# Adaptive layernorm, dilated local attention and SwiGLU on one core: a new instruction order from a search that uses delays read from the trace

## The chip, the cores and the metric

The kernel runs on one core of a Trainium2 chip. The core has a matrix engine (PE; its weight loads are shown apart as PEld), a vector engine (DVE), a scalar engine (ACT), a general one (POOL) and a queue engine (SP) that issues nearly all transfers of this kernel. Each runs its own instructions in the order in which they were written and waits for the others through semaphores. The metric is the time of one execution on the device in microseconds (us); lower is better.

## The reference

One layer over 2048 positions of 512 values: a conditioning vector gives six modulation vectors; then layernorm, attention, residual, layernorm, gated feed-forward (FFN), residual.

```python
x = A_x
mod = (_silu(c) @ w_mod).reshape(c.shape[0], 6, 1, -1)
sa, ca, ga, sb, cb, gb = ...
h = _layernorm(x, axis=-1) * (1 + ca) + sa
x = x + ga * _A_ref(h, A_wqkv, A_wo)      # 32 heads of 16; each position sees itself and
                                          # the positions 2, 4, ... 14 before it (W=8, dil=2)
h = _layernorm(x, axis=-1) * (1 + cb) + sb
x = x + gb * _B_ref(h, B_w1, B_w3, B_w2)  # (silu(h @ w1) * (h @ w3)) @ w2, F = 1792
```

## The kernel before

The positions are cut into 16 tiles of 128 (T = 0 to 15). `_build` records 1118 operations, each with an engine, what it reads and writes, and pools of buffers. `Program.place` then puts them in the order that the list ORDER gives (numbers of operations, over all engines) and gives each pooled value the buffer that SLOTS names; `synchronize` works out the waits from that, also the one for the last user of a buffer that is taken again; `emit` writes each engine's operations in that order. So ORDER and SLOTS decide everything about the schedule: nothing is reordered at run time. GATES adds three waits to late weight loads.

Names used below, with the lines where the work is issued:

- Opening: 24 warm-up matmuls (L518), the modulation columns (L504, L487), two blocks of gate columns (L531, weights `wm_g`) and their spreading over partitions (L541), whose results scale `wo` (L946, DVE) and `w2` (L952).
- First layernorm, QKV groups of tiles [0,1], [2,3], [4-7], [8-11], [12-15]: statistics on DVE (L555, L556), the power on POOL (L565), the normalised tile on DVE (L571, L576, called nm), then a transpose: on PE with an eviction by ACT (L636, L644) for the first three groups, by a transfer (L124) with a modulation by ACT in place (L621) for the last two. The result is `h`.
- Projections (PE): q and k (L691) in pieces q0 to q19 and k0 to k19, v (L711) by tile; ACT evicts them (L700, L701, L721). v goes through one of three buffers to DRAM (`v_scratch`), from where it is read back shifted (eight rows per position) into `vsh`, four transfers per tile (vl).
- Attention by pairs of tiles: products of q and shifted k on DVE (L742, pq), their sums over each head by PE (L752, lg, in a quarter of the columns per matmul), maximum, subtraction (L764, L769), exponential on ACT (L782), sum, reciprocal, product on DVE (L794, L796, L797), a transpose on PE (L807, at) that ACT evicts (L811), products with v on DVE (L827, av), their sum on PE (L855, ac, a quarter of the columns again), eviction by ACT (L861), a transposing transfer (ot), `wo` on PE (L867) and the residual on DVE (L871, rs), which also gives the sum for the second layernorm.
- Second layernorm, FFN groups 0 to 5 of tiles [0,1], [2,3], [4-7], [8-11], [12,13], [14,15]: mean on POOL (L586), squares on ACT (L590), the rest on POOL (L596, L597, L599), normalisation on ACT (L601), transposes on PE for groups 0 and 1, by transfers (tr14 to tr20) and L621 for the others.
- FFN: 14 blocks per group, numbered f0 to f83; each has four matmuls for the gate and four for the up part (L883; 256 or 512 positions wide), a silu on ACT (L889) and a product on DVE (L892). Two halves of seven matmuls per tile (L921, z) give the output, four of 10 and 4 for the last two tiles (L909); DVE adds x (L931) and SP stores it (zo).

PSUM has eight banks, one per matmul result in flight, so a late eviction holds up a later matmul that takes its bank.

Of the kernel before, what the change touches and what calls it, by code (L numbers as in the profile page):

```python
# [272 lines left out]
def _build(p, A_x, A_wqkv, A_wo, B_w1, B_w3, B_w2, c, w_mod, out):  # L273
# [752 lines left out]
]  # L1026
SLOTS = [
# [48 lines left out]
```

## Time and profile before

| what | us |
|---|---|
| runs shown: median (lowest to highest) of 3 | 243.57 (243.03 to 244.15) |
| the profiled execution, its time | 242.82 |
| its span, first to last instruction | 241.1 |
| PE busy / idle in the span | 230.4 / 10.7 |
| DVE busy | 179.6 |
| ACT busy | 138.7 |
| mean granted clock of PE | 1.0 |

In the rows, "sb_x<-sb_y" is what is written and read, "x8" how many instructions, and what stands in brackets is the idle time of that engine before the row and what ended it. Rows that merge several instructions of one line give their start and their length. A few matmul records are missing, which shows as a row with one matmul fewer than its block has. "SPq" is SP's queue: its rows show the issue of a transfer, not its landing.

### The profile page before, as it was taken

Reading aid. Unit: us, or ns where it says so; the run is one execution under the profiler, and the core shown is the slowest. Engines: PE = TensorE matmul, PEld = TensorE weight load, DVE = VectorE, ACT = ScalarE, POOL = GpSimd, SP = SyncE. Lnnn points to the kernel's source line nnn. Section 1 sums busy time; section 2 is a strip of 40 time slices with the busy share of each in tenths; the row PEclk is TensorE's granted clock in tenths of the full one; section 3 lists DMA queues with packets and bytes.
Section 4 is the critical chain, followed back from the end, with each engine's and each line's share of the span. In section 5 each row is a group of like instructions: output and inputs, shape, how many; then the busy total and the mean of one; then the engine's idle time right before and its main releaser. Section 6 shows DMA issues by size and latency. Waiting matters only on the chain.

```text
span 241.1 us, 4538 instructions
## 1 busy us (share of the span) xinstructions
PE 230.4 (96%) x1781; PEld 136.8 (57%) x1806; DVE 179.6 (75%) x279; ACT 138.7 (58%) x267; POOL 30.9 (13%) x66
## 2 busy tenths in 40 slices
PE   7988999979999999999799999999999999999995
PEld 4856454544587685564345444444565584485874
DVE  5697999979989999898999999764565044423542
ACT  2296497688999744955964578646537253140300
POOL 4332060004001000250005301001001000000000
PEclk9999999999999999999999999999999999999999
DMA  6999999999979996693893882253220300000103
GB/s 222 370 327 327 163 262 234 287 282 343 331 134 253 283 270 115 160 272 99 213 256 119 195 197 46 66 141 98 76 79 0 46 0 0 3 22 0 48 0 109
DMA packets 46317, 38.85 MB, mean 161 GB/s; under 512 B 21704, under 2 KB 37080, under 8 KB 46296
## 3 DMA queue, kind: packets, MB, share of 16 engines
q1 hardware_dynamic: 46288, 38.56, 62.5%
q8 instruction: 14, 0.23, 0.4%
q14 instruction: 7, 0.06, 0.1%
q10 hardware_dynamic: 8, 0.00, 0.0%
HBM read 29.62 MB, written 4.21 MB: 140 GB/s over the span
## 4 chain that ended last, share of the span: by engine, by line
PE 50%; ACT 1%; DMA 1%; issue 1%; DVE 0%; SPq 0%
PE pall L883 30%; PE pall L921 12%; PE pall L867 3%; PE pall L909 3%; DMA sb_h<-sb_xn 1%; ACT sb_h L621 1%; PE pall L855 1%; PE pall L752 1%; PE pall L807 0%; ACT sb_al L811 0%; DVE sb_o L931 0%; SPq L124 0%
## 5 line engine op out<-in xcount | busy, mean ns | idle before, releaser
L883 PE MATMUL pall<-sb_h,sb_w 128*128 128x256 bf16 (+1 forms) x665 | 101.8, 307 | 1.0 <-ACT sb_h L621 0.6
L883 PEld LDWEIGHTS pall<-sb_h,sb_w 128*128 128x128 bf16 x672 | 64.8, 98 | 36.2 <-issue 1.5
L892 DVE TENSOR_TENSOR sb_hh<-sb_sg,pall 128x256 bf16<-128x256 bf16 (+1 forms) x84 | 40.4, 505 | 32.1 <-PE pall L883 32.0
L889 ACT ACTIVATE sb_sg<-pall 128x256 bf16<-128x256 f32 (+1 forms) x84 | 36.2, 455 | 43.4 <-PE pall L883 37.3
L921 PE MATMUL pall<-sb_w,sb_hh 128*128 128x512 bf16 x189 | 43.7, 379 | 0.4
L742 DVE TENSOR_TENSOR sb_pq<-sb_q,sb_kT 128x4096 bf16<-128x4096 bf16 x16 | 36.3, 2282 | 0.0
L921 PEld LDWEIGHTS pall<-sb_w,sb_hh 128*128 128x128 bf16 x196 | 19.1, 98 | 21.0
L691 PE MATMUL pall<-sb_h,sb_wqkv 128*128 128x512 bf16 (+1 forms) x159 | 30.3, 336 | 0.1
L827 DVE TENSOR_TENSOR sb_vsh<-sb_vsh,sb_al 128x4096 bf16<-128x4096 bf16 x12 | 27.3, 2286 | 2.4 <-ACT sb_al L811 2.2
L621 ACT ACTIVATE sb_h<-sb_h,sb_modc 128x512 bf16<-128x512 bf16 (+1 forms) x24 | 16.3, 733 | 13.0 <-DMA sb_h<-sb_xn 13.0
L691 PEld LDWEIGHTS pall<-sb_h,sb_wqkv 128*128 128x128 bf16 x160 | 15.1, 98 | 12.2 <-ACT sb_h L644 0.5
L931 DVE TENSOR_TENSOR sb_o<-pall,sb_x 128x512 bf16<-128x512 f32 (+1 forms) x18 | 10.9, 627 | 11.8 <-PE pall L921 8.7
L586 POOL TENSOR_SCALAR sb_nm<-sb_sx 128x2 f32<-128x2 f32 x8 | 3.7, 465 | 115.9 <-DVE sb_x L871 115.9
L590 ACT ACTIVATE sb_xn<-sb_x,sb_nm 128x512 bf16<-128x512 bf16 x16 | 11.4, 714 | 11.7 <-POOL sb_nm L586 11.7
L867 PE MATMUL pall<-sb_wo,sb_ot 128*128 128x512 bf16 x60 | 15.0, 379 | 1.1 <-DMA sb_ot<-sb_ac 0.5
L711 PE MATMUL pall<-sb_wqkv,sb_h 128*128 128x512 bf16 x58 | 15.0, 379 | 0.3 <-issue 0.2
L644 ACT ACTIVATE sb_h<-pall,sb_modc 128x256 bf16<-128x256 bf16 (+1 forms) x18 | 9.9, 616 | 8.6 <-DVE sb_modc L509 6.7
L601 ACT ACTIVATE sb_xn<-sb_x,sb_nb,sb_rs 128x512 bf16<-128x512 bf16 x16 | 12.6, 806 | 3.7 <-POOL sb_nb L599 3.7
L871 DVE SCALAR_TENSOR_TENSOR sb_x<-pall,sb_x 128x512 bf16<-128x512 f32 x16 | 11.0, 688 | 2.3 <-PE pall L867 2.3
L701 ACT ACTIVATE sb_kT<-pall 128x512 bf16<-128x512 f32 x16 | 9.6, 606 | 4.7 <-PE pall L691 4.7
L555 DVE BATCH_NORM_STATS2 sb_st<-sb_x 128x6 f32<-128x512 bf16 x16 | 10.4, 678 | 1.3 <-DMA sb_x<-in_A_x_dram 1.3
L721 ACT ACTIVATE sb_v<-pall 128x512 bf16<-128x512 f32 x16 | 9.6, 612 | 2.4 <-DMA v_scratch_dram<-sb_v 2.3
(87 smaller groups left out, 208.6 us busy)
## 6 DMA issues: line engine op xcount, KB each, us to landing
sb_vsh<-v_scratch_dram SPq DMA_DIRECT2D x48, 256.0 KB, 4.6
sb_vshx<-v_scratch_dram SPq DMA_DIRECT2D x16, 256.0 KB, 4.3
sb_w<-in_B_w_dram SPq DMA_DIRECT2D x6, 512.0 KB, 5.6
sb_w<-in_B_w_dram SPq DMA_DIRECT2D x6, 384.0 KB, 6.0
v_scratch_dram<-sb_v SPq DMA_DIRECT2D x16, 128.0 KB, 5.9
out_dram<-sb_o SPq DMA_DIRECT2D x14, 128.0 KB, 1.9
sb_wqkv<-in_A_wqkv_dram SPq DMA_DIRECT2D x6, 256.0 KB, 6.0
sb_x<-in_A_x_dram SPq DMA_DIRECT2D x4, 256.0 KB, 6.3
```

The lines of the kernel that those rows point to most:

```text
L590: p.op("act", lambda e, vn=vn, T=T: e.activation(vn.at[:], x_sb[:, T, :], ACT.Square, bias=nm[:, T, :], accum_out=var[:, T, :]), c_act(512 ...
L601: p.op("act", lambda e, vn=vn, T=T: e.activation(vn.at[:], x_sb[:, T, :], ACT.Identity, bias=nb[:, T, :], scale=rs[:, NT + T, :]), c_act(5 ...
L621: return e.activation(vh.at[:, ft, 0:n * P], vh.at[:, ft, 0:n * P], ACT.Identity, bias=modc[:, 8 * which + ft:8 * which + ft + 1], scale=m ...
L691: ins = e.matmul(bank(vp)[:, j * n:(j + 1) * n], wqkv[:, t, col:col + P], vh.at[:, t, 0:n], start=(t == ORDER[0] and j == 0), stop=(t == O ...
L711: ins = e.matmul(bank(vp), vh.at[:, t, tt * P:(tt + 1) * P], wqkv[:, t, 2 * D:3 * D], start=(t == ORDER[0]), stop=(t == ORDER[-1]))
L742: return e.tensor_tensor(vp.at[:], in0, in1, ALU.mult)
L827: return e.tensor_tensor(v_w, v_w, a_w, ALU.mult)
L867: ins = e.matmul(bank(vy), vt.at[:, ft, :], wo[:, ft, :], start=(ft == 0), stop=(ft == KT - 1))
L883: ins = e.matmul(bank(vp)[:, 0:n], wt[:, t, fi * P:(fi + 1) * P], vh.at[:, t, 0:n], start=(t == 0), stop=(t == KT - 1))
L889: p.op("act", lambda e: e.activation(vt.at[:, 0:n], bank(vgp)[:, 0:n], ACT.Silu), c_act(n), k, r=[vgp], w=[vt], table="silu")
L892: p.op("dve", lambda e: e.tensor_tensor(vh_.at[:, 0:n], vt.at[:, 0:n], bank(vup)[:, 0:n], ALU.mult), c_dve(n), k, r=[vt, vup], w=[vh_])
L921: ins = e.matmul(bank(vz), vhh[fi].at[:, tt * P:(tt + 1) * P], w2[:, fi, :], start=(fi == 0), stop=(fi == NF - 1))
```

## The change

ORDER and SLOTS are replaced; all else is the same text, GATES included. Each engine issues the same instructions with the same shapes. The list was found by a search that began at the old one and reckoned with delays and late transfers read from the old order's trace.

```diff
@@ GATES, ORDER and SLOTS @@
 GATES = [-1, -1, -1, -1, -1, -1, -1, -1, -1, 1, -1, -1, -1, -1, -1, 1, -1, -1, 2, -1]
 ORDER = [
     8, 9, 10, 0, 20, 21, 22, 3, 4, 1, 2, 16, 17, 23, 24, 25, 26, 27, 28, 29, 30, 31, 32, 34, 33, 18, 59, 60, 61, 62, 63, 64, 11, 12,
-    13, 65, 55, 19, 56, 5, 6, 7, 57, 58, 66, 67, 68, 69, 70, 71, 72, 73, 74, 75, 76, 77, 78, 79, 80, 81, 82, 91, 38, 92, 93, 94, 96,
-    97, 98, 99, 95, 101, 35, 14, 105, 83, 100, 84, 42, 40, 85, 102, 106, 86, 103, 104, 87, 39, 89, 88, 141, 143, 142, 144, 145, 90,
+    13, 65, 55, 19, 56, 5, 36, 6, 7, 57, 58, 66, 67, 68, 69, 70, 71, 72, 73, 74, 75, 76, 77, 78, 79, 80, 81, 82, 91, 38, 92, 93, 94,
+    96, 97, 98, 99, 95, 101, 35, 14, 105, 83, 100, 84, 42, 40, 85, 102, 106, 86, 103, 104, 87, 39, 89, 88, 15, 141, 124, 119, 120,
...
 ]
 SLOTS = [
-    7, 0, 1, 2, 3, 4, 5, 6, 0, 1, 2, 3, 4, 5, 6, 0, 7, 1, 2, 3, 4, 5, 6, 0, 7, 3, 4, 5, 6, 0, 1, 1, 0, 2, 0, 0, 7, 3, 4, 6, 1, 2, 0,
+    7, 0, 1, 2, 3, 4, 5, 6, 0, 1, 2, 3, 4, 5, 6, 7, 0, 1, 2, 3, 4, 5, 6, 7, 0, 3, 4, 5, 6, 0, 1, 1, 0, 2, 3, 0, 4, 0, 7, 1, 0, 2, 1,
...
```

What this means on the engines, at the places that the prediction speaks of (operations by the names above, in their order on that engine):

```
PE, between the two blocks of gate columns (L531)
  before  transposes of tr4 and tr5, k4, q6, v2, then L531
          (L636 x10, L691 256-wide x16, L711 x4)
  after   q6, v3, spread of gate 1, q4, k10, k9, q8, then L531
          (L691 256-wide x8, L711 x4, L541 x4, L691 256-wide x8, L691 512-wide x12)
SP    before  x12-15, wo, wo, wm_g of block 2, ...
      after   x12-15, wo, wo, wo, wm_g of block 2, ...
SP    before  tr6, v2, tr6, w1, vl0, tr6, tr6, vl0 ... vl1
      after   v2, tr6 x4, then vl1 and vl0 mixed, eight in a row
PE    before  lg5, lg4, wo0, wo1, k17, q17, ...   (QKV group of tiles 12 to 15 begins with k17)
      after   lg4, lg5, q12, wo0, wo1, k16, q16, ...
ACT   before  ac0, ac1, tr9, tr9, tr9, k14, v7, k15, tr9, v9, v8, q14, exp of tiles 2 and 3
      after   ac0, ac1, v10, q14, k14, tr9, v8, k13, tr9, tr9, q12, tr9, exp of tiles 2 and 3
SP    after   tr8, tr8, tr8, v6, w1, ot0, v10, ot1
              (v6 frees the buffer that v8 takes; tr9 is the eviction of tr8)
POOL  before  FFN group 2: var of pair 1, power, product, mean of pair 2, ...
      after   mean of pair 2 stands before the power of pair 1
PE, unbroken stretches of L752 and L855
  before  (lg1 lg0) (lg2 ac0 lg3 ac1) (lg5 lg4) (lg6 ac3 lg7 ac2) (ac5) (ac4 lg8 lg9 ac7 ac6)
          (ac9 lg11 lg10 ac8) (lg12 ac10 lg13 ac11) (lg14 lg15) (ac13 ac12) (ac15 ac14)
  after   (lg0 lg1) (lg2 ac0 lg3 ac1) (lg4 lg5) (lg6 ac3) (lg7 ac2) (lg9 ac5) (lg8 ac4) (ac7) (ac6)
          (ac9 lg11 lg10 ac8) (ac11 lg12 lg13 ac10) (lg14 lg15) (ac13 ac12) (ac15 ac14)
DVE   before  av13, av12, sums, av14, rs13, rs12, f43, zo5, av15
      after   av13, f41, av12, zo2, zo6, rs13, rs12, av15, av14
SP    before  vl14, ot13, ot12, vl15 x4, tr18, tr18, zo6, zo7, ot15, ot14
      after   vl15, vl12, ..., ot13, ot12, vl14 x4, tr18, tr18, ot15, ot14
PE    after   wo13, wo12, f47, f47, f54, f46, f46, z11, ac15, ac14, f51, f54, z15, f43, f44, wo14
```

120 rows, old and new, of tables (ORDER, SLOTS) are left out of this document.

## The prediction

> **What bounds the kernel now.** I read the page's first two parts first, then the engines' busy time by stretch, PE's waits, and PE's timeline around each wait.
>
> ```profile
> PE 230.4 (96%) x1781; PEld 136.8 (57%) x1806; DVE 179.6 (75%) x279; ACT 138.7 (58%) x267; POOL 30.9 (13%) x66
> ```
>
> ```profile
> 8.43:62.20 53.77, 50.40 (x441) 28.21 (x450) 48.99 (x80) 41.20 (x77) 11.57 (x19) 1.00 1.13 284
> 62.20:116.50 54.30, 52.16 (x489) 34.99 (x493) 51.31 (x70) 39.99 (x80) 6.18 (x12) 1.00 0.83 211
> 116.50:178.50 62.00, 61.42 (x395) 30.04 (x402) 49.71 (x62) 38.37 (x69) 7.98 (x12) 1.00 0.55 136
> 178.50:238.49 59.99, 59.69 (x394) 38.76 (x397) 24.05 (x50) 17.58 (x41) 1.30 (x4) 1.00 0.08 22
> ```
>
> (Columns: stretch, length, then busy time of PE, PEld, DVE, ACT, POOL; granted clock; DMA share, GB/s.) PE sets the end at full clock. It is idle 3.37 us before 62.2, 2.14 in the next stretch, 0.58 and 0.30 in the last two. Operations stay the same, so a new order can only win back those 5.5 us in the first two, and can lose anywhere. DVE is idle only 54.30 - 51.31 = 2.99 us in the second stretch: a second bound close behind.
>
> ```profile
> 18.10 0.54 PE L531 MATMUL pall<-sb_csT_bf,sb_wm_g 128*128 128x1 bf16 x16 [0.63 <-DMA sb_wm_g<-in_w_mod_dram]
> 22.71 0.54 PE L531 MATMUL pall<-sb_csT_bf,sb_wm_g 128*128 128x1 bf16 x16 [0.88 <-DMA sb_wm_g<-in_w_mod_dram]
> 49.47 1.06 PE L752 MATMUL pall<-sb_pq,sb_E 128*32 128x256 bf16 x32 [0.85 <-ACT sb_kT L701]
> 50.99 1.67 PE L867 MATMUL pall<-sb_wo,sb_ot 128*128 128x512 bf16 x7 [0.46 <-ACT sb_h L621]
> 65.59 0.40 PE L807 MATMUL pall<-sb_ident,sb_attn 128*128 128x128 bf16 x4 [0.18 <-ACT sb_sg L889]
> 96.84 1.02 PE L867 MATMUL pall<-sb_wo,sb_ot 128*128 128x512 bf16 x4 [0.51 <-DMA sb_ot<-sb_ac]
> 115.33 0.61 PE L855 MATMUL pall<-sb_vsh,sb_ind 128*32 128x512 bf16 x8 [0.67 <-DVE sb_vsh L827]
> 116.50 5.99 PE L883 MATMUL pall<-sb_h,sb_w 128*128 128x512 bf16 x27 [0.55 <-ACT sb_h L621]
> ...
> 149.31 6.04 PE pall L921 x28
> ```
>
> These are PE's real waits (the number in brackets). A 512-wide matmul occupies 6.04 / 28 = 0.216 us. Where a row has one matmul too few (x7 of 8, x27 of 28), the unrecorded first one fills 0.216 of the gap, so 0.46 is 0.24 and 0.55 is 0.33. Together: gates 1.51, the 49-51 us pair 1.09, the four later ones 0.18 + 0.51 + 0.67 + 0.33 = 1.69. After 116.5 PE has nothing to win.
>
> **The change, part by part.** Only ORDER and SLOTS differ: the same instructions in another order on each engine and SP, in other buffers.
>
> **1. Gate columns (L531).** Between the two gate blocks stood ten transposes, sixteen 256-wide and four 512-wide projection matmuls; now sixteen 256-wide (0.108 each), four spreads and sixteen 512-wide: 1.7 + 0.2 + 3.5 = 5.4 us. From about 18.5 the second block is reached near 23.9; its weights landed at 22.71. One more piece of wo is now ahead of them on SP (128 KB at the stretch's 284 GB/s, an estimate of 0.46 us), which still fits: 0.88 is gone. The first block has two more transposes ahead, so 0.5 of its 0.63 may stay. Gain 1.0 (bounds 0.4 to 1.5).
>
> What was late next is the first attention products:
>
> ```profile
> 19.26 2.78 ACT L644 ACTIVATE sb_h<-pall,sb_modc 128x512 bf16<-128x512 bf16 x4 [1.00 <-PE pall L636]
> 27.70 0.59 ACT L721 ACTIVATE sb_v<-pall 128x512 bf16<-128x512 f32 x1
> 28.18 0.60 ACT L701 ACTIVATE sb_kT<-pall 128x512 bf16<-128x512 f32 x1
> ...
> 24.01 4.49 DVE L742 TENSOR_TENSOR sb_pq<-sb_q,sb_kT 128x4096 bf16<-128x4096 bf16 x2
> ```
>
> ACT now starts the four L644 evictions when PE has made the eight transposes, near 18.0, ends near 20.8, then moves q2, k4, q4, q6 at 0.48 each (the distance of two starts): 22.7. DVE's two products start near 23 instead of 24.01, so attention moves ahead with PE. On SP the four transposes of group 3 go out back to back, then all reads of tiles 0 and 1, with no weight load between.
>
> **2. The pair at 49-51 us.** The logits of tiles 4 and 5 now follow four projections and precede q12; their banks are freed by q14, not k14, which ACT does earlier. The wait that can replace both is PE's for the last QKV group's h: ACT evicts it (L621, four times) in the order first piece, v8, k13, two pieces, q12, last piece, where it stood as three together and one:
>
> ```profile
> 46.62 2.23 ACT L621 ACTIVATE sb_h<-sb_h,sb_modc 128x512 bf16<-128x512 bf16 x3 [0.47 <-DMA sb_h<-sb_xn]
> 50.18 0.81 ACT L621 ACTIVATE sb_h<-sb_h,sb_modc 128x512 bf16<-128x512 bf16 x1
> ...
> v_scratch_dram<-sb_v SPq DMA_DIRECT2D x16, 128.0 KB, 5.9
> sb_h<-sb_xn SPq DMA_TRANSPOSE x20, 3.9
> sb_ot<-sb_ac SPq DMA_TRANSPOSE x16, 3.3
> ```
>
> The first L867 now takes the bank that v8 leaves, so v8 decides twice. Its SBUF buffer is freed by v6's store, which stands on SP behind that group's four transposes. With these issued by 39 to 41 the store lands near 46.6, after its median 5.9; then 0.48 + 0.48 + 1.42 + 0.48 + 0.71 us of ACT end near 50.2, just as PE reaches k16. New wait 0.2 (bounds 0 and 0.8): gain 0.9.
>
> **3. Waits at 65, 97, 115 and 116 us.** The last two hang on FFN group 2's layernorm:
>
> ```profile
> 108.75 1.52 ACT L601 ACTIVATE sb_xn<-sb_x,sb_nb,sb_rs 128x512 bf16<-128x512 bf16 x2 [2.01 <-POOL sb_nb L599]
> 110.83 2.44 DMA sb_h<-sb_xn
> 113.29 2.94 ACT sb_h L621 x4
> ```
>
> POOL's mean of the second pair (L586) is put ahead of the first pair's power, and the residuals L871 of tiles 6 and 7 come 1.4 and 2.0 us of DVE work earlier. So ACT's 2.01 us wait mostly goes and h is ready with PE's arrival. DVE runs av9 and av8 after the same amount of work as before, so it is ahead by what parts 1 and 2 gave it. At 97 us the wo matmuls wait for the same kind of transposes in the same order; I leave 0.4 there. Gain 1.3 (bounds 0 and 1.7).
>
> **4. More changes of tile mode.** L752 and L855 use a quarter of the columns per matmul. They stood in 11 unbroken stretches; now in 14 (logits 9 and 8 and ac7, ac6 are spread out).
>
> ```profile
> 126.87 4.48 PE L883 MATMUL pall<-sb_h,sb_w 128*128 128x512 bf16 x20
> 131.28 0.62 PE L752 MATMUL pall<-sb_pq,sb_E 128*32 128x256 bf16 x16
> ...
> 132.60 0.60 PE L855 MATMUL pall<-sb_vshx,sb_ind 128*32 128x512 bf16 x8
> 133.36 0.81 PE L883 MATMUL pall<-sb_h,sb_w 128*128 128x512 bf16 x3 [0.16 <-issue]
> ```
>
> Twenty matmuls of 0.216 from 126.87 reach 131.19, the stretch starts at 131.28: 0.09. Its last block takes 0.44 to 133.04; the next matmul (one unrecorded) began at 133.36 - 0.216 = 133.14: 0.10. So 0.2 a stretch, and three more cost 0.6 (bounds 0, where waits cover them, and 1.0). The Trainium skill, "TensorEngine Tiling (Array Packing)", Tiling Modes, says that a change of tiling mode drains TensorE. Taken as a whole matmul's tail at either edge it would be an estimated 0.33 a stretch and 1.0 in all, and the sum 0.4 worse; the trace shows the edges, but smaller.
>
> **5. Last attention tiles.** av15 now precedes av14, its reads go out first, and ot15 and ot14 stand on SP behind the two transposes of FFN group 4. From the end of wo12 PE has nine blocks of four 512-wide FFN matmuls (7.8), two L921 halves (3.0), ac15 and ac14 (1.1): 11.9 us until wo14. Meanwhile the chain is DVE, POOL, two ACT squares, three POOL, two ACT normalisations, four transposes:
>
> ```profile
> L871 DVE SCALAR_TENSOR_TENSOR sb_x<-pall,sb_x 128x512 bf16<-128x512 f32 x16 | 11.0, 688 | 2.3 <-PE pall L867 2.3
> L586 POOL TENSOR_SCALAR sb_nm<-sb_sx 128x2 f32<-128x2 f32 x8 | 3.7, 465 | 115.9 <-DVE sb_x L871 115.9
> L590 ACT ACTIVATE sb_xn<-sb_x,sb_nm 128x512 bf16<-128x512 bf16 x16 | 11.4, 714 | 11.7 <-POOL sb_nm L586 11.7
> L601 ACT ACTIVATE sb_xn<-sb_x,sb_nb,sb_rs 128x512 bf16<-128x512 bf16 x16 | 12.6, 806 | 3.7 <-POOL sb_nb L599 3.7
> L597 POOL TENSOR_TENSOR sb_rs<-sb_rs,sb_cst 128x2 f32<-128x2 f32 x8 | 5.6, 701 | 0.7
> L599 POOL TENSOR_TENSOR sb_nb<-sb_nm,sb_rs 128x2 f32<-128x2 f32 x8 | 5.1, 639 | 0.6
> 45.68 2.50 SPq L124 DMA_TRANSPOSE sb_ot<-sb_ac  x2
> ```
>
> (Columns of the grouped rows: busy us, mean ns of one, idle before.) That is 0.7 + 0.5 + 1.4 + (0.5 + 0.7 + 0.64) + 1.6 + 4 x 1.25 + 3.3 - 1.25 for the last to land = 13.4 us at medians; landings were quicker this late, for DMA is down to half the load of the first stretch, so I take 12.9. PE waits for ot14 about 1.0 (bounds 0 and 2.5). It is new: no wait stood here.
>
> **Sum.** -1.0 - 0.9 - 1.3 + 0.6 + 1.0 = -1.6 us. The span becomes 239.5 and the profiled execution's 242.82 becomes 241.2. The median of the runs shown (243.57) lies 0.75 above that execution, and the same 1.6 taken from it gives 242.0. I forecast 241.6, between the two; this footing, 243.2 without change, serves the rivals too. Up to 8.4 us the order is the old one, and after PE's last L909 one L931 and its store follow as before: nothing either way.
>
> **Rivals.**
>
> *Bigger gain (0.10).* Parts 2 and 5 at their good ends: no wait for k16 or ot14. 1.6 + 0.2 + 1.0 = 2.8 us, 240.4. For it: ACT has 12.6 us idle in the first stretch. Against: SP's queue is in order.
>
> *DVE keeps the pace (0.15).* DVE's 2.99 us of idle time in 62-116 us are waits for PE and ACT; if the new order leaves them, only part 1's gain lasts, and half of it is paid back in parts 4 and 5: -0.4, 242.8. For it: 94% busy DVE. Against: its first products start earlier.
>
> *As many waits at other places (0.12).* The delays were read from the old order; in a new one other transfers are late, and the change does not do what it says: 243.2.
>
> *Slower (0.18).*
>
> ```profile
> L721 ACT ACTIVATE sb_v<-pall 128x512 bf16<-128x512 f32 x16 | 9.6, 612 | 2.4 <-DMA v_scratch_dram<-sb_v 2.3
> ...
> 40.48 2.91 SPq L124 DMA_TRANSPOSE sb_h<-sb_xn  x2
> ```
>
> The place is ACT's eviction of v8. The last two transposes of that group are issued until 43.39 now. If they keep that time, v6's store goes out at 43.4 and lands after its median 5.9 at 49.3, 2.7 later than I reckon; under the load of that stretch (DMA share 1.13) it may be as much again, and 4 us is the middle. ACT runs in order, so h, the next exponentials and DVE's sums all wait, and PE at its first L867 and at k16 with them: -1.6 + 4.0 = +2.4, 245.6. It outweighs the gain from a landing after about 48.2. For it: v evictions have waited 2.3 us for such stores. Against: DVE makes the four inputs of those transposes about three us earlier than before.
>
> **How the numbers follow.** The forecast has 0.45. By about 0.5% (1.2 us, what a measurement here can tell): faster = 0.45 + 0.10 = 0.55; within = 0.15 + 0.12 = 0.27; slower = 0.18. The likeliest case alone spans 240.6 to 242.5 (parts 1 to 5 at moderate bounds). The range 239.9 to 245.2 holds the big gain and the no-change cases and half of the slower one.
>
> **What would show it.** Right: no wait before the second L531; the first L742 near 23; FFN's first L883 near 62.7 with lg6 and ac3 done before it; no 2 us POOL wait of L601 near 105; some 14 tiled stretches; a wait of about 1 us at an L867 near 170. Wrong: an ACT wait on v_scratch_dram of over 2 us near 46, or PE waits for L827 or L621 of over 1 us between 62 and 160.

## The result, and the profile after

The new order is faster: median 241.35 us (240.89 to 242.30) against 243.54 (242.81 to 244.15), seven runs each; ratio 0.9928, 95% interval 0.9902 to 0.9954. Measured once more beside the experiments it gave 241.93 against 242.91, ratio 0.9968 (0.9950 to 0.9985). So it gains between 0.15% and 1.0%. The profiled execution took 241.33 us against 242.82, its span is 239.6 against 241.1: 1.5 us less. Among the experiments below, eleven of the twelve timed runs of "silus first" and five of the twelve of "mean on DVE" had a granted clock of 0.992 or 0.993 instead of 1.0, so these two are judged by their profiles, taken at 1.0, and not by their times.

First the page's engine line and the busy time by stretch (columns as before: stretch, length, PE, PEld, DVE, ACT, POOL, granted clock, DMA share, GB/s). The second stretch ends where PE begins FFN group 2, 111.95 now and 116.3 before, so that the first two together hold the same work; the first alone does not, for the new order is further on at 62.2.

```profile
PE 231.9 (97%) x1806; PEld 135.9 (57%) x1806; DVE 179.2 (75%) x279; ACT 138.8 (58%) x267; POOL 30.0 (13%) x66
```

```profile
8.43:62.20 53.77, 53.18 (x481) 29.32 (x479) 51.02 (x79) 44.11 (x83) 9.24 (x18) 1.00 1.15 276
62.20:111.95 49.75, 49.56 (x462) 33.45 (x460) 48.79 (x70) 36.76 (x74) 5.16 (x12) 1.00 1.02 234
111.95:175.00 63.05, 60.64 (x386) 27.74 (x383) 50.32 (x64) 36.75 (x64) 10.10 (x13) 1.00 0.57 131
```

PE's idle time fell from 3.37 to 0.59 us in the first stretch and from 2.14 to 0.19 in the second; in the third, where there was little, 2.41 has appeared. PE's timeline shows the places:

```profile
9.18 2.46 PE L691 MATMUL pall<-sb_h,sb_wqkv 128*128 128x256 bf16 x20 [0.37 <-DVE sb_st L555]
...
18.29 0.54 PE L531 MATMUL pall<-sb_csT_bf,sb_wm_g 128*128 128x1 bf16 x16
...
24.11 0.54 PE L531 MATMUL pall<-sb_csT_bf,sb_wm_g 128*128 128x1 bf16 x16
...
50.21 2.97 PE L691 MATMUL pall<-sb_h,sb_wqkv 128*128 128x512 bf16 x13
...
92.33 0.61 PE L855 MATMUL pall<-sb_vsh,sb_ind 128*32 128x512 bf16 x8 [0.19 <-DVE sb_vsh L827]
...
111.96 2.33 PE L883 MATMUL pall<-sb_h,sb_w 128*128 128x512 bf16 x10
...
156.93 3.62 PE L883 MATMUL pall<-sb_h,sb_w 128*128 128x512 bf16 x16
162.20 1.04 PE L883 MATMUL pall<-sb_h,sb_w 128*128 128x512 bf16 x4 [1.66 <-ACT sb_sg L889]
...
165.52 0.62 PE L855 MATMUL pall<-sb_vsh,sb_ind 128*32 128x512 bf16 x8 [0.23 <-ACT sb_sg L889]
...
171.81 1.90 PE L867 MATMUL pall<-sb_wo,sb_ot 128*128 128x512 bf16 x8 [0.51 <-DMA sb_ot<-sb_ac]
```

Neither gate block (18.29, 24.11), nor k16 (50.21), nor the first block of FFN group 2 (111.96) waits any more. That last block began at 116.50 - 0.22 = 116.28 before, after the same work, so 4.3 us were won by then. From there to the end the new order takes 2.8 longer. A wait of 1.66 that the prediction does not have stands at f46's second block; with 0.23 at ac14 and 0.51 at wo14, and 0.16 more for each (worked out further down), that is 2.9.

What was late there is seen on the other engines. POOL, DVE, ACT and SP's queue, new order:

```profile
157.92 2.19 POOL L586 TENSOR_SCALAR sb_nm<-sb_sx 128x2 f32<-128x2 f32 x1 [16.87 <-DVE sb_x L871]
161.75 0.54 POOL L596 TENSOR_SCALAR sb_rs<-sb_var 128x2 f32<-128x2 f32 x1 [1.64 <-ACT sb_xn L590]
```

```profile
157.75 2.29 DVE L827 TENSOR_TENSOR sb_vshx<-sb_vshx,sb_al 128x4096 bf16<-128x4096 bf16 x1
159.95 2.29 DVE L827 TENSOR_TENSOR sb_vsh<-sb_vsh,sb_al 128x4096 bf16<-128x4096 bf16 x1
```

```profile
160.14 0.72 ACT L590 ACTIVATE sb_xn<-sb_x,sb_nm 128x512 bf16<-128x512 bf16 x1 [4.14 <-POOL sb_nm L586]
...
161.57 1.06 ACT L889 ACTIVATE sb_sg<-pall 128x512 bf16<-128x512 f32 x2
163.38 1.52 ACT L601 ACTIVATE sb_xn<-sb_x,sb_nb,sb_rs 128x512 bf16<-128x512 bf16 x2 [0.75 <-POOL sb_nb L599]
```

```profile
164.92 3.11 SPq L124 DMA_TRANSPOSE sb_h<-sb_xn  x2
168.08 2.57 SPq L124 DMA_TRANSPOSE sb_ot<-sb_ac  x2
```

POOL's mean over 128x2 values lasted 2.19 us and ended at 160.11, when DVE's av15 had ended (160.04). ACT's two squares wait for it, and the silu of f47, in order behind them, frees the bank that PE needs. The same in the order before, there on the last product of the layernorm (L599); the second POOL row is the same mean of group 4 as above, with no product beside it:

```profile
106.71 2.00 POOL L599 TENSOR_TENSOR sb_nb<-sb_nm,sb_rs 128x2 f32<-128x2 f32 x1
...
162.52 0.22 POOL L586 TENSOR_SCALAR sb_nm<-sb_sx 128x2 f32<-128x2 f32 x1 [15.26 <-DVE sb_x L871]
```

```profile
106.38 2.28 DVE L742 TENSOR_TENSOR sb_pq<-sb_q,sb_kT 128x4096 bf16<-128x4096 bf16 x1
```

Theory, from here on "lock": a POOL step that comes up while DVE runs one of its 2.28 us products (L742, L827, both inputs in SBUF) cannot get through until that product ends. In the traces of all 13 kernels 76 of the layernorms' POOL steps began while such a product was running: 72 ended 0.05 to 0.08 us after it, and four powers 0.55 to 0.56 after it; none of the other 541 took more than 1.01. The Trainium skill, "SBUF — State Buffer", section "SBUF: two separate sides", says that DVE and the POOL engine share a pair of SBUF ports, as an exclusive lock for a whole instruction, and counts DVE operations with two SBUF inputs among those that take it; the traces agree, for these steps end 0.05 to 0.08 us after the product. The other way round they show no lock: a product that DVE begins while a POOL step is still running keeps its time (new order: the product of 53.95 took 2.28 beside the power of 53.67 to 54.37).

### The profile page after: what moved, and what is told of

It reads as the page before. It is cut to its first block, busy times and chain, and to the rows that moved or that the text cites. A ratio compares the mean times of both kernels' runs of the same rounds, so it can differ in the third digit from the quotient of the medians.

```text
span 239.6 us, 4572 instructions
## 1 busy us (share of the span) xinstructions
PE 231.9 (97%) x1806; PEld 135.9 (57%) x1806; DVE 179.2 (75%) x279; ACT 138.8 (58%) x267; POOL 30.0 (13%) x66
## 4 chain that ended last, share of the span: by engine, by line
PE 79%; DMA 6%; DVE 5%; SPq 4%; ACT 2%; POOL 2%; issue 1%; DVEq 0%
PE pall L883 36%; PE pall L921 16%; PE pall L691 7%; PE pall L867 6%; DMA sb_x<-in_A_x_dram 5%; SPq L124 4%; PE pall L711 4%; PE pall L752 3%; PE pall L855 3%; PE pall L909 3%; DVE sb_pq L742 2%; DMA sb_ot<-sb_ac 1%; DVE sb_vsh L827 1%; POOL sb_nm L586 1%; DVE sb_st L555 1%
## 5 line engine op out<-in xcount | busy, mean ns | idle before, releaser
L883 PE MATMUL pall<-sb_h,sb_w 128*128 128x256 bf16 (+1 forms) x672 | 102.9, 308 | 1.7 <-ACT sb_sg L889 1.7
L883 PEld LDWEIGHTS pall<-sb_h,sb_w 128*128 128x128 bf16 x672 | 64.8, 98 | 38.1 <-ACT sb_sg L889 2.1
L889 ACT ACTIVATE sb_sg<-pall 128x256 bf16<-128x256 f32 (+1 forms) x84 | 35.7, 453 | 50.9 <-PE pall L883 49.0
L921 PE MATMUL pall<-sb_w,sb_hh 128*128 128x512 bf16 x196 | 45.1, 379 | 0.0
L742 DVE TENSOR_TENSOR sb_pq<-sb_q,sb_kT 128x4096 bf16<-128x4096 bf16 x16 | 36.4, 2283 | 0.0
L691 PE MATMUL pall<-sb_h,sb_wqkv 128*128 128x512 bf16 (+1 forms) x160 | 31.1, 336 | 0.4 <-DVE sb_st L555 0.4
L827 DVE TENSOR_TENSOR sb_vsh<-sb_vsh,sb_al 128x4096 bf16<-128x4096 bf16 x12 | 27.3, 2285 | 0.0
L691 PEld LDWEIGHTS pall<-sb_h,sb_wqkv 128*128 128x128 bf16 x160 | 14.6, 97 | 12.1 <-DVE sb_st L555 0.6
L867 PE MATMUL pall<-sb_wo,sb_ot 128*128 128x512 bf16 x64 | 15.8, 379 | 0.5 <-DMA sb_ot<-sb_ac 0.5
L711 PE MATMUL pall<-sb_wqkv,sb_h 128*128 128x512 bf16 x64 | 16.0, 379 | 0.0
L861 ACT ACTIVATE sb_ac<-pall 128x512 bf16<-128x512 f32 x16 | 9.4, 597 | 7.0 <-PE pall L855 6.8
L555 DVE BATCH_NORM_STATS2 sb_st<-sb_x 128x6 f32<-128x512 bf16 x16 | 10.5, 680 | 1.4 <-DMA sb_x<-in_A_x_dram 1.4
```

Of the source, the lines that this page charges most:

```text
L555: o = p.op("dve", lambda e, T=T: e.bn_stats(st[:, T, :], x_sb[:, T, :]), 595, ("st", T), r=[vx[T]], w=[vs])
L691: ins = e.matmul(bank(vp)[:, j * n:(j + 1) * n], wqkv[:, t, col:col + P], vh.at[:, t, 0:n], start=(t == ORDER[0] and j == 0), stop=(t == O ...
L711: ins = e.matmul(bank(vp), vh.at[:, t, tt * P:(tt + 1) * P], wqkv[:, t, 2 * D:3 * D], start=(t == ORDER[0]), stop=(t == ORDER[-1]))
L742: return e.tensor_tensor(vp.at[:], in0, in1, ALU.mult)
L827: return e.tensor_tensor(v_w, v_w, a_w, ALU.mult)
L867: ins = e.matmul(bank(vy), vt.at[:, ft, :], wo[:, ft, :], start=(ft == 0), stop=(ft == KT - 1))
```

## The experiments

All start from the new order, and each was profiled and timed beside the order before (medians of before: 243.13 beside "mean on DVE", "three steps on DVE", "silus first" and "gate early"; 242.91 beside "the same again", "combined", "v6 late" and "mean back"; 243.22 beside the last three). The opening differs by up to 1.3 us between executions (waits for `wm_s` of 0 to 1.27), so stages are compared by PE's own times, the start of a block's first weight load:

| kernel | q10 | f1 | f31 | f47 | wo14 | f47 to wo14 | span | ratio to before (95%) |
|---|---|---|---|---|---|---|---|---|
| new order | 24.48 | 62.19 | 111.95 | 156.71 | 171.80 | 15.09 | 239.6 | 0.9928 (0.9902-0.9954) |
| the same again | 24.22 | 61.68 | 111.45 | 156.22 | 171.28 | 15.06 | 239.1 | 0.9968 (0.9950-0.9985) |
| mean on DVE | 24.40 | 61.76 | 112.01 | 156.78 | 171.32 | 14.54 | 239.1 | 0.9950 (0.9915-0.9986) |
| three steps on DVE | 24.01 | 61.69 | 113.14 | 158.78 | 172.18 | 13.40 | 240.0 | 0.9875 (0.9830-0.9920) |
| silus first | 24.36 | 61.91 | 112.64 | 157.41 | 172.49 | 15.08 | 240.3 | 0.9997 (0.9967-1.0026) |
| combined | 25.26 | 62.73 | 112.62 | 157.39 | 169.81 | 12.42 | 237.6 | 0.9875 (0.9845-0.9904) |
| gate early | 25.62 | 63.17 | 114.12 | 158.88 | 174.24 | 15.36 | 242.0 | 0.9998 (0.9976-1.0020) |
| v6 late | 24.74 | 66.25 | 116.81 | 161.57 | 176.72 | 15.15 | 244.5 | 1.0141 (1.0115-1.0168) |
| mean back | 25.03 | 62.45 | 113.64 | 158.66 | 173.73 | 15.07 | 241.5 | 1.0015 (0.9986-1.0043) |
| product and mean | 23.98 | 61.72 | 114.68 | 160.44 | 175.65 | 15.21 | 243.5 | 1.0060 (1.0036-1.0083) |
| product alone | 24.34 | 61.79 | 112.06 | 158.78 | 173.93 | 15.15 | 241.7 | 1.0008 (0.9987-1.0029) |
| more cuts | 24.07 | 62.95 | 114.92 | 159.89 | 174.38 | 14.49 | 242.2 | 1.0001 (0.9974-1.0028) |

**The new order again.**

> The new order itself once more, beside the others on the same chip: ratio to the order before near 0.993, waits of about 1.7 at L883 near 162, 0.2 at L855 and 0.5 to 0.9 at wo14, in whatever the earlier stages do.

As expected, with 1.65, 0.23 and 0.49 at the three late places.

**The mean of group 4 on DVE.**

```diff
-        p.op("pool", lambda e: e.tensor_scalar(nm[:, i:i + n, 0], ...
+        p.op("dve" if i == 12 else "pool", lambda e: e.tensor_scalar(nm[:, i:i + n, 0], ...
```

> The new order, with one operation on another engine: the mean (L586) of FFN group 4 is made on DVE, right behind rs12, instead of on POOL. Theory 'lock': POOL cannot run a step while DVE runs one of its 2.28 us products; that mean took 157.92 to 160.11, ending with DVE's av15 (160.03), where the other means took 0.22. Without it ACT's squares start near 158.1 instead of 160.14, the silu behind them near 159.6 instead of 161.57, and PE's waits of 1.66 (L883 near 162) and 0.23 (L855 near 165.5) go. POOL's later steps of this group still run beside av14, so the group's transposes, and ot14 behind them, come at most 0.8 earlier, and the wait at wo14 grows from 0.51 to about 1.3: span about 238.6 (-1.0). Rival 'pace': PE is simply ahead of what the other engines can follow there, and the waits turn up elsewhere: span 239.6, no change.

ACT, POOL and DVE, and PE of this kernel:

```profile
158.13 0.72 ACT L590 ACTIVATE sb_xn<-sb_x,sb_nm 128x512 bf16<-128x512 bf16 x1 [2.07 <-DVE sb_nm L586]
...
163.36 1.52 ACT L601 ACTIVATE sb_xn<-sb_x,sb_nb,sb_rs 128x512 bf16<-128x512 bf16 x2 [2.74 <-POOL sb_nb L599]
164.78 0.57 ACT L889 ACTIVATE sb_sg<-pall 128x512 bf16<-128x512 f32 x1
```

```profile
160.44 2.62 POOL L597 TENSOR_TENSOR sb_rs<-sb_rs,sb_cst 128x2 f32<-128x2 f32 x1
```

```profile
160.22 2.28 DVE L827 TENSOR_TENSOR sb_vsh<-sb_vsh,sb_al 128x4096 bf16<-128x4096 bf16 x1
```

```profile
165.50 0.62 PE L855 MATMUL pall<-sb_vsh,sb_ind 128*32 128x512 bf16 x8 [1.97 <-ACT sb_sg L889]
```

The squares come at 158.13, two us earlier, and the wait at 162 is gone, as the lock has it. But the power then ran into av14 (160.22 to 162.50): 2.62 instead of 0.70, so ACT normalised at 163.36 as before, and f46's silu behind it (164.78) held the bank of ac14. The stage is 0.5 shorter, half of what was expected: the wait moved to ac14, not to wo14.

**Three of the four steps on DVE.** POOL keeps the power, in a pause of DVE.

```diff
-  DVE   rs13, rs12, av15, av14                          POOL  mean, var, power, product
+  DVE   rs13, rs12, mean, av15, var, product, av14      POOL  power
```

> The new order, with the mean, the variance step (L596) and the last product (L599) of FFN group 4 on DVE, the first ahead of av15, the other two between av15 and av14; only the power (L597) stays on POOL, at a time when DVE runs no long product. Theory 'lock': squares near 158.1, normalisation near 161.4 instead of 163.38, transposes 1.7 to 2 us earlier, ot15 and ot14 right behind their evictions; all three late waits (1.66, 0.23, 0.51) go: span 237.3 (-2.3). Rival 'pace': no change, 239.6. If the lock costs only the mean, and ot14 is held by the queue's order, it comes out like the kernel with the mean alone, near 238.6.

```profile
172.19 1.90 PE L868 MATMUL pall<-sb_wo,sb_ot 128*128 128x512 bf16 x8 [0.85 <-DMA sb_ot<-sb_ac]
```

(One line further down in this file than L867.) The two ACT waits are gone, the stage is 1.7 shorter (2.3 expected), and one wait is left, at wo14. The span of 240.0, where 237.3 was expected, also holds waits of 0.65, 0.48 and 0.70 near 89, 98 and 120, ahead of the edit.

**Silus first: the order of ACT alone.**

```diff
-  ACT   f43, square 13, square 12, f47, f54, norm 12, ...
+  ACT   f43, f47, f54, square 13, square 12, norm 12, ...
```

> The new order, with ACT's silus of f47 and f54 ahead of the two squares of FFN group 4 (the mean stays on POOL). Rival 'ACT's order': PE's wait of 1.66 came only from the silu standing behind the squares; with it ahead the wait goes and nothing else is late: span 238.0 (-1.6). Theory 'lock': the wait near 162 goes too, but the squares, the transposes and ot14 are as late as before, so PE waits the more at wo14 (about 2.3 instead of 0.51): span 239.6, within 0.3.

```profile
166.22 0.61 PE L855 MATMUL pall<-sb_vsh,sb_ind 128*32 128x512 bf16 x8 [2.06 <-ACT sb_sg L889]
...
172.49 1.90 PE L867 MATMUL pall<-sb_wo,sb_ot 128*128 128x512 bf16 x8 [0.50 <-DMA sb_ot<-sb_ac]
```

The stage takes 15.08 us, the same to a hundredth: the wait only changed its place (ac14 instead of f46; it was expected at wo14). f46's silu still stands behind the late normalisation and holds ac14's bank, and ot14 comes as late as before. So this order on ACT is not the cause; what comes late to ACT is.

**Combined.** The three steps on DVE, and two moves:

```diff
-  SP    tr18 (tile 13), tr18 (tile 12), ot15, ot14
+  SP    tr18 (tile 12), tr18 (tile 13), ot15, ot14
-  PE    k2, k0, k0 (2nd piece), q0, ..., q2
+  PE    k2, k0, q0, q2, k0 (2nd piece), ...
```

> The kernel with the mean, the variance step and the last product of group 4 on DVE, and two more moves: on SP the transpose of tile 12 ahead of that of tile 13 (the queue stood until ACT had normalised tile 13, 164.9, though tile 12 was done 0.7 earlier), so that both transposes and ot15 and ot14 behind them go out 0.7 to 1.8 earlier and the wait of 0.85 at wo14 goes; and in the opening the second pieces of k0 stand behind the first pieces of q0 and q2, so that the 0.3 to 0.4 us that PE waits there for h goes. Theory 'lock and queue order': from the first f47 block to wo14 12.4 to 12.6 us (15.1 in the new order, 13.4 with the three steps on DVE alone), ratio to before 0.983. Rival: wo14 then waits for something else (ac14's eviction), and only the opening gains: 13.2, ratio 0.987.

```profile
165.03 1.68 PE L883 MATMUL pall<-sb_h,sb_w 128*128 128x512 bf16 x7 [0.21 <-DVE sb_hh L892]
...
169.81 1.90 PE L867 MATMUL pall<-sb_wo,sb_ot 128*128 128x512 bf16 x8
```

The stage takes 12.42, as expected (the bracket of 0.21 is the unrecorded eighth matmul), and wo14 no longer waits. The ratio, 0.9875, is short of the 0.983 expected. The move in the opening shows nothing: from k2 to q10 15.95, against 16.29 and 15.98 in the two profiles of the new order. At 239.3 us this kernel is faster than the order before by 1.0% to 1.6%, and than the new order, timed beside it, by 2.6 us: it beats both.

**The second gate block four projections earlier** (part 1 undone).

```diff
-  PE    q4, k10, k9, q8, L531 (block 2), q10
+  PE    q4, L531 (block 2), k10, k9, q8, q10
```

> The new order, with the second block of gate columns (L531) on PE put back to right behind q4, four projections earlier, so that PE reaches it near 21.9 while its weights land near 23.3 to 23.8. Prediction's theory 'PE sets the end': a wait of 1.4 to 1.9 us shows there and is carried to the end in full: span 241.0 to 241.5. Rival 'pace': the late waits (1.66, 0.23, 0.51) are time in which PE is ahead of the other engines, so they shrink by as much as PE is later: span 239.6 to 240.0.

```profile
22.85 0.54 PE L531 MATMUL pall<-sb_csT_bf,sb_wm_g 128*128 128x1 bf16 x16 [1.09 <-DMA sb_wm_g<-in_w_mod_dram]
```

The weights landed earlier than I took, so the wait is 1.09. It is carried on: the late waits are 1.65, 0.24 and 0.78, not smaller. "Pace" falls: time won at 24 us is not paid back because others cannot follow. The ratio to before is 0.3% to 0.7% higher than the new order's; f31 is 2.2 to 2.7 later, 1.0 to 1.3 more than q10, which is in waits of 0.78 near 91 and 0.24 more at ac6 that other executions also have.

**v6's store some 4 us later** (the slower rival).

```diff
-  SP    tr8 x3, v6, w1, ot0, v10, ot1
+  SP    tr8 x3, w1, ot0, v10, ot1, v6
```

> The new order with v6's store put on SP behind w1, ot0, v10's store and ot1, some 4 us later. It went out at 42.85 and landed 2.9 later, at 45.75, and ACT evicted v8 into its buffer at 46.19: 0.44 to spare. The prediction's slower rival as a mechanism: the store goes out near 46.5 and lands near 49.5 (2.9 to 3.5 later); ACT waits for it about 3.2, h of the last QKV group and the exponentials are as much later, and PE waits at the first wo block or at k16, 2.5 to 3.2 in all: span +2.5 to +3.2. Rival: ACT has 12 us idle in this stretch and catches up, PE loses under 1.0.

New order, SP and ACT, and then this kernel, SP and ACT, and PE:

```profile
42.85 0.58 SPq L124 DMA_DIRECT2D v_scratch_dram<-sb_v  x1
```

```profile
46.19 0.59 ACT L721 ACTIVATE sb_v<-pall 128x512 bf16<-128x512 f32 x1
```

```profile
46.96 0.58 SPq L124 DMA_DIRECT2D v_scratch_dram<-sb_v  x1
```

```profile
49.02 0.60 ACT L721 ACTIVATE sb_v<-pall 128x512 bf16<-128x512 f32 x1 [2.42 <-DMA v_scratch_dram<-sb_v]
```

```profile
49.72 1.89 PE L867 MATMUL pall<-sb_wo,sb_ot 128*128 128x512 bf16 x8 [1.16 <-DVE pall L769]
...
52.74 4.49 PE L691 MATMUL pall<-sb_h,sb_wqkv 128*128 128x512 bf16 x20 [1.14 <-ACT sb_h L621]
...
61.39 0.27 PE L636 MATMUL pall<-sb_ident,sb_xn 128*128 128x128 bf16 x2 [0.48 <-ACT sb_xn L601]
```

ACT waits 2.42 for the store, PE at the first wo, at k16, and then again at the second layernorm of group 0, which ACT normalises late. From q10 to f1 PE takes 41.51, 3.8 to 4.1 more than the new order (37.71 and 37.46), and more than the 2.5 to 3.2 expected, which left out the second layernorm. The mechanism is as the prediction's rival has it and ACT does not catch up.

**The mean of group 2's second pair back behind the first pair's power and product** (part 3 undone).

```diff
-  POOL  var 1, mean 2, power 1, product 1
+  POOL  var 1, power 1, product 1, mean 2
```

> The new order with POOL's mean (L586) of the second pair of FFN group 2 put back behind the power and product of the first pair, as it stood before. In the new order it ran 98.93 to 99.14, ACT's squares of that pair began at 99.18, the last L621 of the group ended at 111.55, and PE took the first L883 of the group at 111.95, so 0.4 is to spare. Prediction's reading 'it only queues behind two short steps': the mean comes about 1.0 later, PE waits 0.6 at that L883: span +0.6. Theory 'lock': it then comes up within 0.1 us of DVE's product of 99.94 to 102.22; where the product has begun first, the mean lasts until its end, the squares begin 3.1 later, and PE waits 2.5 to 3.5 there: span +2.5 to +3.5. (If the mean wins that race, the two theories agree.)

```profile
101.13 0.20 POOL L599 TENSOR_TENSOR sb_nb<-sb_nm,sb_rs 128x2 f32<-128x2 f32 x1
101.29 0.22 POOL L586 TENSOR_SCALAR sb_nm<-sb_sx 128x2 f32<-128x2 f32 x1
```

```profile
113.87 5.99 PE L883 MATMUL pall<-sb_h,sb_w 128*128 128x512 bf16 x27 [0.43 <-ACT sb_h L621]
```

In this execution the mean got in 0.06 ahead of DVE's product (101.35), and PE waited 0.2 (the unrecorded 28th matmul fills 0.22 of the bracket). So this run did not tell the theories apart. The median is 1.5 us above that of the new order beside it; the profile shows more than the edit can explain (waits of 0.97 in the opening and 0.75 near 90, both ahead of it), and this stays open.

**The same with the product ahead, and the product ahead alone.**

```diff
-  DVE   sm8, f18, f14, pq11, f15                    (both kernels)
+  DVE   sm8, pq11, f18, f14, f15
-  POOL  var 1, mean 2, power 1, product 1           (first kernel only)
+  POOL  var 1, power 1, product 1, mean 2
```

> The new order with POOL's mean of the second pair of FFN group 2 behind the first pair's power and product, and DVE's product for tile 11 (L742) two short products earlier, so that it has begun before the mean is due (0.6 earlier than in the kernel with the mean alone put back, where the mean got in 0.06 ahead of it and lasted 0.22). Theory 'lock': the mean (or, if that stands first, the product L599) lasts until the end of that L742, some 1.5 to 2.1 us; ACT's squares of that pair begin 1.5 to 2 later than with the mean alone put back, and PE's wait at the group's first L883 is 1.5 to 2.5 (0.43 there). Rival 'no lock, only queues': the small steps take 0.2 to 0.7 as elsewhere and the wait stays at 0.4 to 0.6.

> The new order with only that product of DVE (L742, tile 11) two short products earlier, the mean where the new order has it, ahead of the power. Theory 'lock': the mean slips in ahead of the product and the squares begin on time; the first pair's product L599 is locked out instead, which ACT needs only 1.2 us later: PE's wait at the group's first L883 is under 0.6, beside 1.5 to 2.5 with the mean behind. Rival 'the two short products made late are what costs': both kernels wait the same.

POOL, DVE and PE, first with the mean behind:

```profile
100.13 2.28 POOL L599 TENSOR_TENSOR sb_nb<-sb_nm,sb_rs 128x2 f32<-128x2 f32 x1
102.38 0.21 POOL L586 TENSOR_SCALAR sb_nm<-sb_sx 128x2 f32<-128x2 f32 x1
```

```profile
100.08 2.28 DVE L742 TENSOR_TENSOR sb_pq<-sb_q,sb_kT 128x4096 bf16<-128x4096 bf16 x1
```

```profile
114.68 6.22 PE L883 MATMUL pall<-sb_h,sb_w 128*128 128x512 bf16 x28 [1.27 <-ACT sb_h L621]
```

then with the mean ahead:

```profile
98.70 0.21 POOL L586 TENSOR_SCALAR sb_nm<-sb_sx 128x2 f32<-128x2 f32 x1
98.87 0.70 POOL L597 TENSOR_TENSOR sb_rs<-sb_rs,sb_cst 128x2 f32<-128x2 f32 x1
99.65 1.73 POOL L599 TENSOR_TENSOR sb_nb<-sb_nm,sb_rs 128x2 f32<-128x2 f32 x1
```

```profile
99.05 2.28 DVE L742 TENSOR_TENSOR sb_pq<-sb_q,sb_kT 128x4096 bf16<-128x4096 bf16 x1
```

```profile
112.06 6.22 PE L883 MATMUL pall<-sb_h,sb_w 128*128 128x512 bf16 x28 [0.27 <-ACT sb_h L621]
...
120.07 1.04 PE L867 MATMUL pall<-sb_wo,sb_ot 128*128 128x512 bf16 x4 [1.78 <-DMA sb_ot<-sb_ac]
```

With DVE's product begun (100.08), L599 lasted 2.28 and the mean came out at 102.38 behind it. With the product as early and the mean ahead, PE waits 0.27 at this L883. The lock holds in a second place, by order alone; PE's wait there is 1.27, less than the 1.5 to 2.5 expected, and 1.0 more than with the mean ahead. A wait of 0.42 at 104.47, for a silu that stands behind the same squares on ACT, comes on top. The totals don't price it: the first kernel also has waits of 0.47 and 0.21 near 89 and 98, ahead of the group's first L883, and both wait at an L867 near 120 for a transposing transfer (0.83 and 1.78; the kernel with three steps on DVE, edited elsewhere, has 0.70 there). So the second kernel, too, is no faster than the order before; whether the moved product causes its 1.78 is open.

**Six more cuts.** ac1, lg5, ac3, ac5, ac4 and ac10 one block later each.

```diff
-  PE    (lg2 ac0 lg3 ac1) q14 ... (lg4 lg5) q12 ... (lg9 ac5) transpose
+  PE    (lg2 ac0 lg3) q14 (ac1) ... (lg4) q12 (lg5) ... (lg9) transpose (ac5)
```

> The new order with six of its 14 unbroken stretches of L752 and L855 cut once more, by one projection, transpose or FFN block each (ac1, lg5, ac3, ac5, ac4 and ac10 stand one block later): 20 stretches. Prediction's price, 0.2 a stretch: PE's work from lg2 (41 us) to ac13 (149 us) takes 1.2 longer, without a wait shown. By the larger price (a whole matmul's tail at either edge, 0.33): 2.0 longer. Rival 'no price' (the edges are hidden by the weight loads that run ahead): under 0.3. A wait at ac1, ac3, ac5, ac4 or ac10's users would come on top and would be seen in brackets.

From lg2 to ac13 PE takes 111.66 against 108.05 in both profiles of the new order: 3.6 more. Waits explain 1.9 of it (wo4 1.12 instead of none, v12 0.26, ac6 0.17 more, each but the last 0.16 dearer than its bracket, see below). That leaves 1.7 for six cuts, 0.29 each; the two that stand clear of other gaps, at ac1 and ac10, cost 0.21 each (5.63 instead of 5.42, 7.36 instead of 7.15). So the price of 0.2 holds there. The 0.33 worked out beside "TensorEngine Tiling (Array Packing)", Tiling Modes, of the Trainium skill is too much for the clear cuts; on the average of the six it is not excluded. (In this execution ot14 landed in time, which makes the last stage 0.6 shorter.)

## Why the prediction was right, and where it was not

The total was forecast well, by two errors that cancel, which is luck: 4.3 us were won by FFN group 2 where parts 1 to 4 make 2.6, and 2.8 lost behind it where part 5 has 1.0. Of the two measurements one (2.2 us) is clear of the 1.2 that the prediction says can be told, the other (1.0) is not.

- **Part 1, gate columns: right, undersized.** The second block came at 24.11 (23.9 forecast), DVE's first products at 23.5 (23). The 0.5 left at the first block did not show, but PE now waits 0.37 in the opening, for h (the bracket names DVE's L555; ACT's eviction of h ends at 9.12, just ahead), which I had not looked at.
- **Part 2, the pair at 49-51: right, for partly wrong reasons.** No wait is left, not even 0.2. v6's store went out at 42.85, not by 41: nearly the time that I gave to the slower rival. It landed 2.9 later, at 45.75, where I took the median of 5.9. Only 0.44 was to spare when ACT evicted v8. PE began FFN's first block at 62.19, 1.7 earlier than before and with lg6 and ac3, 0.9 us of work, already done; 62.7 was forecast.
- **Part 3, the four later waits: right in place, the mechanism misread.** 0.19 is left of 1.69. I took ACT's wait of 2.01 near 106 for POOL's order and let the mean ahead of the power remove it. Its row (L599, 2.00) was a step under DVE's product of 106.38. The place of the mean matters through that: PE waited 0.27 with it ahead and 1.27 with it behind once the product had begun, and about 0.2 where it slipped in first. In the new order the second pair's variance step is still held there (1.49 at 100.78), but early enough that PE does not wait.
- **Sizes of parts 1 to 3: a reading of brackets.** A bracket counts from the end of a matmul's row. Such a row lasts 0.38, but the next matmul begins 0.216 after the start. Before 162.20 sixteen matmuls from 156.93 fill the time to 160.39, so 1.81 is lost where the bracket says 1.66. With 0.16 on each of eight waits (1.3) the 4.29 of the order before were some 5.6; less what is left (0.37, 0.19 and 0.3 for their ends) and 0.6 for part 4 that makes 4.1, close to the 4.3 measured.
- **Part 4, three more stretches: right as far as tested,** 14 of them, 0.2 for a clear cut.
- **Part 5, last attention tiles: the step that failed.** It lets PE wait 1.0 for ot14, by a chain whose first POOL step, the mean, costs 0.5. That mean lasted 2.19, because av15 was put right behind rs12. The chain's terms as written add up to 13.1, not 13.4, and the 12.9 taken from it is a choice; the stage took 15.1. Beside the mean (1.7 more) the four transposes held the queue longer (5.7 instead of 5.0), and the first of them, tile 13's, could go out only when ACT had normalised both tiles (164.9). Most of the loss then showed not at wo14 (0.51) but at f46 (1.66) and ac14 (0.23), through the silus that stand behind the squares on ACT. All three go with the steps taken out from under the product and the SP queue turned round. The 465 ns that I used for the mean were an average of seven of 0.22 and one of 2.19: the row that showed the lock was in the trace, hidden in a mean.
- **The rivals.** "DVE keeps the pace" falls with the early gate block, whose wait is carried to the end. "Slower" has the right mechanism and, for a store that lands near 49, the right price (4.0 forecast, 3.8 to 4.1 by f1). Its condition, a landing after about 48.2, was 2.4 us away from the 45.75 of the new order. "As many waits at other places" came true in part: 2.4 us of new waits stand behind 156, though mostly through POOL's late step and not through late transfers. Of "bigger gain" one half came true (no wait at k16), the other (none at ot14) did not.

## What to carry to other kernels

Before a small POOL step is priced from a grouped row, look at its single rows: if some are ten times longer, see what DVE ran beside them, and keep long two-input DVE products from starting just ahead of such a step, or put the step on DVE. A wait found in one place on an in-order engine should be followed to what came late; moving only the work behind it moves the wait (15.08 against 15.09 us here). Add to each bracket before a pipelined matmul the part of the row that overlaps the next start, here 0.16 us.

## What the runs showed of the hardware

- POOL steps of 0.2 us that came up while a DVE product with two SBUF inputs (2.28 us) was under way ended 0.05 to 0.08 after it, however much of it was left, and so lasted up to 2.3. The power (0.70) lasted 2.62 when av14 began 0.22 ahead of it, and ended 0.56 after it. Beside DVE operations that read PSUM they kept their time: the mean of 98.93 took 0.21 while a DVE multiplication with a PSUM input (L797) ran from 98.68 to 99.37.
- v stores of 128 KB landed 2.9 and 3.5 us after their issue at 42.85 and 45.27 in the new order, and 2.0 after that at 46.96 with v6 late, where the median over the run before was 5.9. When such a store let ACT go on 2.8 us later (49.02 instead of 46.19), PE lost about 4.
